# Chunked linear attention with an FFN: from a 128-token chunk step to a 64-token one, four more dummy products, and a new order of all pieces

## The chip, the core and the metric

The kernel runs on one core of a Trainium2 chip. The metric is the device time of one execution in microseconds (us); the time before is the median of three runs. A profile is the trace of one execution; its span runs from the first to the last instruction.

## What is computed

The reference, cut to what matters. For each of 4 batches and 8 heads, 768 tokens go through a decayed linear attention with a state of 16 x 32; then come a layer norm without bias and a two-layer ReLU network with a residual. All inputs and outputs are fp32.

```python
for c in range(nc):                      # chunks of 32 tokens
    cum = np.cumsum(la, axis=-1)         # la = log of the clipped decay a
    L = np.exp(cum[..., :, None] - cum[..., None, :]) * causal
    M = np.einsum('bhin,bhjn->bhij', Cc, Bc) * L
    y_intra = np.einsum('bhij,bhjd->bhid', M, xc)
    y_inter = np.einsum('bhin,bhnd->bhid', Cc, state) * np.exp(cum)[..., None]
    y[:, :, sl] = y_intra + y_inter
    state = exp(sum(la)) * state + sum_j(Bc_j x_j decay_from_j)
xn = (x - mu) / np.sqrt(var + 1e-06) * g_ln          # x = y, heads side by side
out = x + np.maximum(xn @ w_ch1, 0.0) @ w_ch2
```

## The kernel before

The 768 tokens are cut into six blocks of 128 (t = 0 to 5), and each block holds all 4 batches and 8 heads. Batches are counted as v (2) x u (2), heads in four pairs q. The work of a block is a set of small functions, called pieces here, each with a short name. The text `ISSUE` lists every piece of every block with its engine (`v` VectorE, `a` ScalarE, `p` GpSimd, `s` the DMA queue of SyncE); it is written out by hand, and each engine executes its instructions in that order. So an instruction that waits holds up everything behind it on its engine.

The pieces of the attention, with their lines in the profile:

- `C`, `cm`, `B`: C and B are multiplied by running decay products, rows `ud` that a DMA spreads over the partitions through DRAM (`ro`, then `ld ud`); block 0 takes these rows from two TensorE products instead (`U`, `ur`, L325 and L330). `cm` holds C twice, once with the odd heads zeroed and once with the even ones.
- `G` (L381, TensorE): the products of C and B, one call for each u. A call has 8 products whose moving operand has 256 columns (the first 64 keys against all 128 queries, two heads) and 8 with 128 columns (the last 64 keys against the last 64 queries). They work on 32x64 tiles of the array, 8 tiles at a time. An fp32 product stands in the trace as two MATMUL instructions, so a call counts 32.
- `R` (L388, VectorE): G times the decay mask `WW`, 128x384, eight times a block. `W` (L162, ScalarE or GpSimd) writes a block's decays into `WW`; `ones` fills it once with the causal mask.
- `I` (L400, TensorE): the state's share of y, 128 columns each, 32 instructions a block. `V` (L415, TensorE): R times x, 128 instructions a block on 64x32 tiles, half of 128 columns and half of 64. `Z` (L427, TensorE): the block's addition to the state, 64 instructions of 64 columns; it writes into a spare third of the banks of y.
- `K`, `S`, `sb` (L432, L441, L445): the state is decayed, added to, and laid out in blocks for the next block's `I`. `be` (L361) scales B for `Z`.

The pieces of the network:

- y is copied out of PSUM (`y`), split into a high and a low fp32r part (`yh`, `yl`), multiplied with the weights' two parts (`h`, L510, six products of up to 512 columns), passed through the ReLU by ScalarE (`hh`, L516), split by VectorE (`hl`, L522) and multiplied with the second weights (`o`, L537 and L538). `T`, `tw`, `tc` bring y into token order for the norm and the residual.
- The weights arrive as 64-bit words and are decoded on the chip by `k0`, `kr` (ScalarE), `k2`, `k3` (VectorE) and `f` (L212), centred by TensorE products (`wc`, `wm`, with `gd` and `gm` as factors) and split (`wh`, `wl`).
- `e`, `x`, `so`, `sm`, `mb`, `sp`, `em` make the decays of all blocks once, near the start. `fill` is a product of zeros that only keeps TensorE busy.

All PSUM tiles come from one pool of eight banks, `banks`: a piece that needs a bank waits until the reader of an earlier tile has released one.

Of the kernel before, what the change touches and what calls it, by code (L numbers as in the profile page):

```python
# [8 lines left out]
F32 = mybir.dt.float32  # L9
# [35 lines left out]
C_COEF = C_COL + P // NH  # L45
C_ID = C_COEF + 3 * P // 4
# [6 lines left out]
def shape_constants():  # L53
# [18 lines left out]
    w = np.concatenate([w[:, 1, :HALF], w[:, 3, HALF:], w[:, 2, :HALF], w[:, 3, :HALF], w[:, 0]], axis=1)  # L72
# [5 lines left out]
def linear_attention_ffn(ctx, tc, xv, a, bt, bn, cn, w1, w2, consts, out):  # L78
# [9 lines left out]
    rp = pool("rp", 12)  # L88
# [6 lines left out]
    cfr = hp.tile([P, 3 * P], F32, tag="hh", name="cfr")  # L95
# [12 lines left out]
    AZ = cp.tile([P, NL + 1], F32, name="AZ")  # L108
    inv = cp.tile([P, NL], F32, name="inv")
    ini = cp.tile([P, NL], F32, name="ini")  # L110
# [3 lines left out]
    WW = [cp.tile([P, NH, PW], F32, name=f"WW{i}") for i in range(NU)]  # L114

# [9 lines left out]
    def load(what, *at, e=nc.sync):  # L125
# [13 lines left out]
        elif what in src:  # L139
# [6 lines left out]
            e.dma_start(dst, src[what][t])  # L146
# [38 lines left out]
    def masks(u, e=nc.scalar):  # L185
        copy(e, WW[u], causal.unsqueeze(1).to_broadcast([P, NH, PW]))

# [63 lines left out]
    emt = cp.tile([P, NT, NB], F32, name="emt")  # L251
    msum = cp.tile([NR, NT, NSUB + 1], F32, name="msum")
    mblk = cp.tile([NR, NB, NT * (NSUB + 1)], F32, name="mblk")
# [11 lines left out]
    def sums_to(what):  # L265
        parts = lambda w: w.rearrange("p t (v u h) -> p v t u h", u=NU, v=NV)
        if what == "p":
            sums[what] = e = banks.tile([P, NT, NR], F32, tag="bank", name="ep")
            todo = [(4 + j, v, parts(e)[:, j]) for j in range(2) for v in range(NV)]
        else:  # L270
            sums[what] = e = banks.tile([P, 4, NT, NU, NH], F32, tag="bank", name="ew")
            todo = [(i, v, e[:, i]) for i in range(4) for v in range(NV)]
        for i, v, dst in todo:
            nc.tensor.matmul(dst[HALF * v:HALF * (v + 1)], cfr[:, i * HALF:(i + 1) * HALF], parts(la)[:, v], start=True, stop=True)

    def decays_to(what):
        nc.scalar.activation(*((pend, sums[what]) if what == "p" else (wt, sums[what])), AF.Exp)
# [7 lines left out]
    def decays_of():  # L285
        nc.scalar.activation(msum, sums["s"][:, :, :NSUB + 1], AF.Exp)

    def apart(e=nc.gpsimd):

        e.tensor_tensor(out=mblk, in0=msum.rearrange("r t i -> r (t i)").unsqueeze(1).to_broadcast([NR, NB, NT * (NSUB + 1)]),  # L290
                        in1=selt[:, P:].unsqueeze(2).to_broadcast([NR, NB, NT * (NSUB + 1)]), op=ALU.mult)

    def spread():

        sums["d"] = emps = banks.tile([P, NB, NT, NSUB + 1], F32, tag="bank", name="emps")
        nc.tensor.matmul(emps.rearrange("p b t i -> p (b t i)"), selt[:, :P], mblk.rearrange("r b c -> r (b c)"), start=True, stop=True)
# [74 lines left out]
    def score(t, u):  # L371

        bs, cm = tiles["bs", t], tiles["cm", t]
        G = [banks.tile([P, 2, PW], F32, tag="bank", name=f"G{t}{u}{q}") for q in range(NQ)]
# [10 lines left out]
    def weighted(t, u, q):  # L385
        R = tiles["R", t, u, q] = rp.tile([P, 2, PW], F32, tag="R", name=f"R{t}{u}{q}")
        flat = lambda v: v.rearrange("p i k -> p (i k)")
        nc.vector.tensor_tensor(out=flat(R), in0=flat(tiles.pop(("G", t, u, q))), in1=flat(WW[u][:, 2 * q:2 * q + 2]), op=ALU.mult)  # L388

    def inter_products(t):  # L390

        c2 = tiles["c2", t].rearrange("p i k -> p (i k)")
        for u in range(NU):
            for g in range(KC):
                tiles["y", t, u, g] = banks.tile([P, NU + 1, P], F32, tag="bank", name=f"yps{t}{u}{g}")
        for u in range(NU):
# [5 lines left out]
    def value(t, u):  # L402

        x = tiles["x", t]
        if t == u == 0:
            for v in range(NV):
                for g in range(KC):
                    tiles["y", t, v, g] = banks.tile([P, NU + 1, P], F32, tag="bank", name=f"yps{t}{v}{g}")
        for j in range(2):
            at = slice(P, PW) if j else slice(0, P)  # L410
            for g in range(KC):
                for k in range(4):
                    for v in range(NV):
                        h, c, p = 4 * g + k, 32 * (k ^ 2 * v), slice(HALF * v, HALF * (v + 1))
                        nc.tensor.matmul(tiles["y", t, v, g][c:c + 32, u, HALF * j:], x[p, (j * NU + u) * NH + h], tiles["R", t, u, h // 2][p, h % 2, at],  # L415
                                         start=(t == u == j == 0), stop=(j == 1), skip_group_check=True)

    def carry(t):

        x, be = tiles["x", t], tiles["be", t]  # L420
        Z = tiles["Z", t] = [tiles["y", t, v, 0][:, NU] for v in range(NV)]
        for u in range(NU):
            for j in range(2):
                for q in range(NQ):
                    for v in range(NV):
                        h0, p = (j * NU + u) * NH + 2 * q, slice(HALF * v, HALF * (v + 1))
                        nc.tensor.matmul(Z[v][32 * q:32 * q + 32, u * 2 * HD:(u + 1) * 2 * HD], be[p, h0:h0 + 2].rearrange("p h n -> p (h n)"),  # L427
                                         x[p, h0:h0 + 2].rearrange("p h d -> p (h d)"), start=False, stop=(j == 1), skip_group_check=True)

    def kept(t, e=nc.vector):  # L430
        S = tiles["K", t] = p1.tile([P, NB, 2 * HD], F32, tag="K", name=f"K{t}")
        e.tensor_tensor(out=S, in0=tiles["S", t - 1], in1=emt[:, t].unsqueeze(2).to_broadcast([P, NB, 2 * HD]), op=ALU.mult)  # L432

    def state_of(t):
        S = tiles["S", t] = p2.tile([P, NB, 2 * HD], F32, tag="S", name=f"S{t}")
        for v, z in enumerate(tiles.pop(("Z", t))):
            s = S[:, v * NU:(v + 1) * NU].rearrange("p u d -> p (u d)")
            if t == 0:
                nc.scalar.copy(s, z)
            else:  # L440
                nc.vector.tensor_tensor(out=s, in0=z, in1=tiles["K", t][:, v * NU:(v + 1) * NU].rearrange("p u d -> p (u d)"), op=ALU.add)  # L441
# [219 lines left out]
```

## Time and profile before

| | us |
|---|---|
| median of 3 runs | 190.68 (190.58 to 190.86) |
| the profiled execution: its time | 190.03 |
| the profiled execution: span of its instructions | 188.3 |
| TensorE busy | 181.6 (96% of the span) |
| VectorE, ScalarE, GpSimd busy | 134.5, 72.9, 51.6 |

The profile's page gives for each engine the time in which it executed something. The span and the time differ by 1.7 us, which lie before the first and after the last instruction. The granted TensorE clock averages 0.997 of full speed.

### The profile page before, as it was taken

The page shows a single profiled execution, that of the slowest core. Times are in us where ns is not written, and L with a number is a line of the kernel's source. Part 1 is how long each engine was busy: PE and PEld are TensorE (multiplying, and loading weights), DVE is VectorE, ACT ScalarE, POOL GpSimd, SP SyncE. Part 2 cuts the span into 40 slices and gives each one's busy share as a digit, 9 for nine tenths or more (in the row PEclk, how much of TensorE's full clock was granted, in tenths as well). Part 3 has the DMA queues.
Part 4 walks back from the last instruction along what each step waited for, and adds up shares of the span by engine and source line. Part 5 has one row for each costly group of instructions (what it writes and reads, how often), then busy time and mean ns, then how long its engine had stood idle before and what let it go on. Part 6 is the DMA issues. An engine that isn't in the chain of part 4 may idle for free.

```text
span 188.3 us, 5714 instructions
## 1 busy us (share of the span) xinstructions
PE 181.6 (96%) x2440; PEld 148.6 (79%) x2440; DVE 134.5 (71%) x302; ACT 72.9 (39%) x148; POOL 51.6 (27%) x65
## 2 busy tenths in 40 slices
PE   8979999999999999999998999999999999999992
PEld 8655589987878778788776887888888888888892
DVE  4899999998986797776984846659607574545841
ACT  7799999719434124421341201233102330034100
POOL 3162646624978941230032530000002000000000
PEclk9999999999999999999999999999999999999998
DMA  5999993843883913572150000363001035100102
GB/s 188 410 370 251 334 376 139 216 136 93 292 285 97 215 42 139 173 252 88 44 151 7 3 0 28 109 193 91 3 0 56 31 141 139 35 20 3 56 28 84
DMA packets 16729, 25.04 MB, mean 133 GB/s; under 512 B 4160, under 2 KB 10688, under 8 KB 16704
## 3 DMA queue, kind: packets, MB, share of 16 engines
q1 hardware_dynamic: 16560, 24.45, 40.3%
q8 instruction: 19, 0.31, 0.7%
q10 hardware_dynamic: 144, 0.23, 0.3%
q14 instruction: 6, 0.05, 0.1%
HBM read 18.06 MB, written 6.62 MB: 131 GB/s over the span
## 4 chain that ended last, share of the span: by engine, by line
PE 92%; ACT 4%; DVE 1%; issue 1%
PE ph L510 37%; PE po L537 23%; PE po L538 12%; PE yps L415 6%; PE G L381 4%; PE idle L556 2%; PE yps L427 2%; PE yps L400 2%; DVE R L388 1%; PE wc L226 1%; PE po L534 1%; ACT WW L162 1%; PE wc L227 1%; ACT raw L207 1%; ACT yh L162 1%
## 5 line engine op out<-in xcount | busy, mean ns | idle before, releaser
L537 PE MATMUL po<-w,hh 128*128 128x512 f32 x184 | 64.9, 396 | 0.1
L516 ACT ACTIVATE hh<-ph 128x512 fp32r<-128x512 f32 (+1 forms) x56 | 28.3, 536 | 74.0 <-PE ph L510 48.9
L510 PE MATMUL ph<-yh,w 128*128 128x512 f32 (+1 forms) x224 | 54.6, 365 | 0.0
L538 PE MATMUL po<-w,hl 128*128 128x256 f32 x184 | 47.9, 281 | 0.0
L522 DVE SCALAR_TENSOR_TENSOR hl<-ph,hh 128x512 fp32r<-128x512 f32 (+1 forms) x56 | 32.2, 604 | 17.1 <-ACT hh L516 17.1
L510 PEld LDWEIGHTS ph<-yh,w 128*128 128x128 f32 x224 | 38.2, 189 | 7.1 <-issue 0.3
L537 PEld LDWEIGHTS po<-w,hh 128*128 128x128 f32 x184 | 33.7, 188 | 7.1 <-ACT y L162 0.4
L538 PEld LDWEIGHTS po<-w,hl 128*128 128x128 f32 x184 | 34.7, 188 | 1.7
L510 PE MATMUL ph<-yl,w 128*128 128x512 f32 (+1 forms) x112 | 31.2, 360 | 0.0
L388 DVE TENSOR_TENSOR R<-G,WW 128x384 f32<-128x384 f32 x48 | 24.6, 546 | 5.6 <-PE G L381 4.9
L547 DVE SCALAR_TENSOR_TENSOR o<-po,rstd,ytok 128x256 f32<-128x256 f32 x24 | 11.5, 477 | 21.2 <-PE po L537 19.1
L510 PEld LDWEIGHTS ph<-yl,w 128*128 128x128 f32 x112 | 20.0, 189 | 3.5
L162 POOL COPY WW<-wt 32x512 f32<-32x512 f32 (+1 forms) x15 | 10.4, 695 | 17.0 <-DVE R L388 16.4
L162 POOL CAST yh<-y 128x512 fp32r<-128x512 f32 x5 | 3.3, 676 | 40.9 <-PE ph L510 33.5
L381 PE MATMUL G<-cm,bs 32*64 32x256 f32 (+1 forms) x384 | 12.0, 335 | 1.7 <-DVE bs L351 1.0
L162 ACT COPY WW<-wt 32x512 f32<-32x512 f32 (+1 forms) x21 | 12.8, 614 | 0.9 <-DVE rstd L501 0.7
L381 PEld LDWEIGHTS G<-cm,bs 32*64 32x64 f32 x384 | 7.4, 131 | 6.0 <-issue 2.4
L212 POOL TENSOR_TENSOR top<-top,raw 128x512 int32<-128x512 int32 x6 | 8.1, 1361 | 14.3 <-ACT WW L162 4.5
L547 DVE SCALAR_TENSOR_TENSOR o<-po,rstd,o 128x256 f32<-128x256 f32 x23 | 11.1, 484 | 0.8
L415 PEld LDWEIGHTS yps<-R,xt 64*32 64x32 f32 x768 | 10.1, 105 | 2.0 <-issue 1.2
L415 PE MATMUL yps<-R,xt 64*32 64x64 f32 (+1 forms) x768 | 11.2, 249 | 0.0
L490 DVE BATCH_NORM_STATS2 st<-ytok 128x6 f32<-128x256 f32 x24 | 9.4, 415 | 0.0
(100 smaller groups left out, 178.2 us busy)
## 6 DMA issues: line engine op xcount, KB each, us to landing
raw<-in_w_dram SPq DMA_DIRECT2D x8, 512.0 KB, 6.1
xt<-in_x_dram SPq DMA_DIRECT2D x6, 512.0 KB, 6.0
scr<-yx SPq DMA_DIRECT2D x6, 512.0 KB, 2.9
ytok<-scr SPq DMA_DIRECT2D x24, 128.0 KB, 3.0
out_dram<-o SPq DMA_DIRECT2D x24, 128.0 KB, 1.7
ud<-scr SPq DMA_DIRECT2D x10, 256.0 KB, 4.0
c<-in_cn_dram SPq DMA_DIRECT2D x6, 256.0 KB, 4.7
b<-in_bn_dram SPq DMA_DIRECT2D x6, 256.0 KB, 3.9
```

The costliest lines, as they stand in the source:

```text
L162: (e.copy if e is nc.scalar else e.tensor_copy)(dst, src)
L212: e.tensor_tensor(out=f, in0=f, in1=words.pop((w, *at))[0], op=ALU.add)
L381: nc.tensor.matmul(G[q][HALF * v:HALF * (v + 1), :, at], bs[r, i0 + HALF * j:i0 + HALF * (j + 1)], cm[r, :, i0 + HALF * j:i0 + P], start=T ...
L388: nc.vector.tensor_tensor(out=flat(R), in0=flat(tiles.pop(("G", t, u, q))), in1=flat(WW[u][:, 2 * q:2 * q + 2]), op=ALU.mult)
L415: nc.tensor.matmul(tiles["y", t, v, g][c:c + 32, u, HALF * j:], x[p, (j * NU + u) * NH + h], tiles["R", t, u, h // 2][p, h % 2, at], start ...
L490: nc.vector.bn_stats(out=st, in_=tiles["ytok", t][:, :, b])
L510: nc.tensor.matmul(ph, W1[m // 4, k][:, s, mc], v[:, k, tok], start=(i == 0), stop=(i == len(cmb) - 1))
L516: nc.scalar.activation(tiles["hh", t, m][:, tok], tiles["ph", t, m, u], AF.Relu)
L522: nc.vector.scalar_tensor_tensor(out=tiles["hl", t, m][:, tok], in0=tiles.pop(("ph", t, m, u)), scalar=0.0, in1=tiles["hh", t, m][:, tok]. ...
L537: both = lambda: nc.tensor.matmul(po, hh, w[:, :, at], start=(m == 0), stop=last, skip_group_check=True)
L538: low = lambda: nc.tensor.matmul(po[:, 0], hl, w[:, 0, at], start=False, stop=False, skip_group_check=True)
L547: nc.vector.scalar_tensor_tensor(out=parts(o), in0=parts(po[:, i]), scalar=tiles["rstd", t][:, b], in1=rest, op0=ALU.mult, op1=ALU.add)
```

## The change

**Blocks 1 to 5 in two halves of 64.** `G` becomes one call a block with 32 products of 128 columns (64 instructions): each 64 queries meet only their own 64 keys. `R` becomes four steps of 128x512, with a mask `WC` that serves all of these blocks; `W` becomes two copies a block in place of six. The earlier keys reach a query through the state, which now has two values a block: `I` multiplies the first 64 queries with the state at the block's start and the last 64 with the state in its middle (64 instructions of 64 columns). `V` becomes 128 instructions of 64 columns, in two calls split by half of the heads. `Z` fills both halves into two PSUM banks of its own; `K`, `S` and `sb` run twice a block. Block 5 gets a `Z` (half), `K`, `S`, `sb` and `be` that it didn't have. Block 0 keeps the old scheme.

**Near the start.** `U` makes 128 columns in place of 512, and `ur` four products of 128 in place of one of 512 (with a new step `rg` on GpSimd). A new step `on` fills `WC` with the causal mask, once on each of VectorE and ScalarE. `ones` stands on ScalarE for both u (one was on VectorE). There are 17 `fill` in place of 13. Several tiles now share the buffers of later ones, and the pool of `R` has 8 buffers in place of 12.

**The order.** `ISSUE` is new as a whole. The core of the diff:

```diff
-            todo = [(i, v, e[:, i]) for i in range(4) for v in range(NV)]
-        for i, v, dst in todo:
-            nc.tensor.matmul(dst[HALF * v:HALF * (v + 1)], cfr[:, i * HALF:(i + 1) * HALF], parts(la)[:, v], start=True, stop=True)
+            todo = [(i, v, slice(0, NT if i < 2 else 1), e[:, i]) for i in range(4) for v in range(NV)]
+        for i, v, t, dst in todo:
+            nc.tensor.matmul(dst[HALF * v:HALF * (v + 1), t], cfr[:, i * HALF:(i + 1) * HALF], parts(la)[:, v, t], start=True, stop=True)
...
+    def decays(t, u=None, e=nc.scalar):
+        if t:
+            for p in (slice(0, SUB), slice(HALF, HALF + SUB)):
+                dst = WC[p].rearrange("p u q (i j k) -> p (u q i) j k", i=2, j=2)[:, :, :, SUB:]
+                src = wt[p, :2, t].rearrange("p j u h -> p (u h) j")
+                copy(e, dst, src.unsqueeze(3).to_broadcast([*src.shape, SUB]))
+            return
...
+    def score(t, u=None):
 
         bs, cm = tiles["bs", t], tiles["cm", t]
+        if t:
+            G = [banks.tile([P, NU, 2, P], F32, tag="bank", name=f"G{t}{q}") for q in range(NQ)]
+            for j in range(2):
+                for u in range(NU):
+                    for q in range(NQ):
+                        r = slice(2 * DS * q, 2 * DS * (q + 1))
+                        for v in range(NV):
+                            at = slice((v * NU + u) * P + HALF * j, (v * NU + u) * P + HALF * (j + 1))
+                            nc.tensor.matmul(G[q][HALF * v:HALF * (v + 1), u, :, HALF * j:HALF * (j + 1)], bs[r, at], cm[r, :, at], start=True, stop=True)
...
-        for u in range(NU):
-            for q in range(NQ):
-                for v in range(NV):
-                    b, r, f = v * NU + u, slice(2 * DS * q, 2 * DS * (q + 1)), slice((q ^ v) % 2 * 2 * HD, ((q ^ v) % 2 + 1) * 2 * HD)
-                    nc.tensor.matmul(tiles["y", t, v, q // 2][f, u], tiles["sbd", t - 1][r, b], c2[r, b * P:(b + 1) * P], start=(u == 0), stop=False, skip_group_check=True)
+        summed(t)
+        for j in range(2):
+            state = tiles["sbd", t, 0] if j else tiles["sbd", t - 1, 1]
+            for u in range(NU):
+                for q in range(NQ):
+                    for v in range(NV):
+                        b, r, f = v * NU + u, slice(2 * DS * q, 2 * DS * (q + 1)), slice((q ^ v) % 2 * 2 * HD, ((q ^ v) % 2 + 1) * 2 * HD)
+                        nc.tensor.matmul(tiles["y", t, v, q // 2][f, u, HALF * j:HALF * (j + 1)], state[r, b], c2[r, b * P + HALF * j:b * P + HALF * (j + 1)],
+                                         start=(u == j == 0), stop=False, skip_group_check=True)
...
-        Z = tiles["Z", t] = [tiles["y", t, v, 0][:, NU] for v in range(NV)]
+        Z = tiles["Z", t] = [banks.tile([P, 2, P], F32, tag="bank", name=f"Z{t}{v}") for v in range(NV)]
         for u in range(NU):
-            for j in range(2):
+            for j in range(1 if t == NT - 1 else 2):
...
-ld:s w1 1 1, k3:v 1 0 0, f:p 1 0 0, fill 12, G 0 1, W:a 0 0, e p, k3:v 1 0 1, k0 1 1 1, k0 2 0, R 0 1 0, f:p 1 0 1, kr 1 1 1, R 0 1 2, G 0 0,
+fill 14, fill 15, W:p 0 1, ld:s w1 1 1, ld:s w1 1 0, on:a 0, k0 1 1 1, k2:v 1 1 1, ld:s late, ld:s w2 0, e p, x p, fill 16, G 0 1, gm:p, k3:v 1 0 0,
```

What the new order does at three places follows as rows of instructions, each engine's in its own order; the number behind a tile's name only tells buffers apart, and line numbers differ between the two kernels. First ScalarE from its first copy on. `WW` from `causal` (`early` in the changed kernel) is `ones`, the step on `cst` is the logarithm of the decays, `top` is `k0` and `raw` is `kr` of the weights. Before:

```order
L162 COPY WW_89<-causal 128x1536
L162 CAST cfr<-cst 128x384
L263 ACTIVATE cst<-cst 128x192
L162 COPY uds<-uds 128x160
L193 ACTIVATE top_142<-raw_137 128x512
L277 ACTIVATE wt<-ew 128x384
L207 ACTIVATE raw_137<-raw_137 128x512
L220 ACTIVATE gd<-cst,gneg 128x128 x2
```

The same place in the changed kernel:

```order
L169 COPY WW_88<-early 128x1536
L169 CAST cfr<-cst 128x448
L169 COPY WW_87<-early 128x1536
L273 ACTIVATE cst<-cst 128x192
L203 ACTIVATE top_134<-raw_106 128x512
L169 COPY uds<-uds 128x160
L217 ACTIVATE raw_106<-raw_106 128x512
L203 ACTIVATE top_179<-raw_127 128x512
L217 ACTIVATE raw_127<-raw_127 128x512
L290 ACTIVATE wt<-ew 128x192
```

A second copy of the mask now stands ahead of the logarithm and of the first `k0`. Next VectorE between the first decay products and block 0's `bs`, on which `G` of block 0 waits (`own` or `own_ini` is `U`, `top` is `k2`, `k3` and `f`). Before:

```order
L325 TENSOR_TENSOR own_159<-uds,cst 128x512
L314 SCALAR_TENSOR_TENSOR uds<-AZ,inv 128x192
L197 TENSOR_SCALAR top_142<-top_142 128x512
L325 TENSOR_TENSOR own_166<-uds,cst 128x512
L341 SCALAR_TENSOR_TENSOR cm_170<-c_162,cst,rows_168 128x512 x2
L197 TENSOR_SCALAR top_182<-top_182 128x512
L351 TENSOR_TENSOR bs_187<-b_180,rows_185 128x512
```

The same place in the changed kernel:

```order
L343 TENSOR_TENSOR own_ini<-uds,cst 128x128
L328 SCALAR_TENSOR_TENSOR uds<-ends 128x192
L207 TENSOR_SCALAR top_134<-top_134 128x512
L169 COPY uds<-uds 128x160
L343 TENSOR_TENSOR own_ini<-uds,cst 128x128
L212 SCALAR_TENSOR_TENSOR top_134<-raw_106,top_134 128x512
L207 TENSOR_SCALAR top_179<-top_179 128x512
L222 ISA top_134<-raw_106,top_134 128x1024
L361 SCALAR_TENSOR_TENSOR cm_193<-c_191,cst,rows_154 128x512 x2
L371 TENSOR_TENSOR bs_196<-b_129,rows_186 128x512
```

Two more weight steps and a copy now stand ahead of `cm` and `bs`, and the two `U` are a quarter as wide. Last TensorE at block 1's first `G`, behind the last product of an `h` (`ph`). Before:

```order
L510 MATMUL ph_503<-yl_394,w_287 128x256
L381 MATMUL G_517<-cm_478,bs_501 64x2x128 x2
L381 MATMUL G_518<-cm_478,bs_501 64x2x128 x2
L381 MATMUL G_519<-cm_478,bs_501 64x2x128 x2
L381 MATMUL G_520<-cm_478,bs_501 64x2x128 x2
L381 MATMUL G_517<-cm_478,bs_501 64x2x64 x2
L381 MATMUL G_518<-cm_478,bs_501 64x2x64 x2
L381 MATMUL G_519<-cm_478,bs_501 64x2x64 x2
L381 MATMUL G_520<-cm_478,bs_501 64x2x64 x2
```

The same place in the changed kernel, where the last four rows come four times in all:

```order
L566 MATMUL ph_559<-yl_407,w_325 128x256
L409 MATMUL G_572<-cm_505,bs_527 64x2x64 x2
L409 MATMUL G_573<-cm_505,bs_527 64x2x64 x2
L409 MATMUL G_574<-cm_505,bs_527 64x2x64 x2
L409 MATMUL G_575<-cm_505,bs_527 64x2x64 x2
```

The wide products of 256 columns are gone, and block 1 has this one call in place of two. In the changed kernel six `h` calls and `Z` of block 0 stand between block 0's `V` and this `G`; before, `Z` and four `h` calls did. From there on TensorE meets the small pieces in stretches with `h` or `o` between them: 15 stretches before, and 15 in the changed kernel from this `G` on plus `Z` of block 0.

## Rows read from the trace of the kernel before

**Rows 1.** The page's first part: busy us (share of the span) xinstructions.

```profile
PE 181.6 (96%) x2440; PEld 148.6 (79%) x2440; DVE 134.5 (71%) x302; ACT 72.9 (39%) x148; POOL 51.6 (27%) x65
```

**Rows 2.** Waits of TensorE over the span: us in total, times, longest.

```profile
PE G L381 <- issue: 0.7, 1, 0.7
```

**Rows 3.** Timeline of TensorE, 10 to 26 us: start, us, instruction xcount [idle before].

```profile
10.10 0.91 PE L381 MATMUL G<-cm,bs 32*64 32x256 f32 x32 [0.95 <-DVE bs L351]
...
13.70 1.12 PE L226 MATMUL wc<-top,gd 128*128 128x512 f32 x2 [0.40 <-POOL top L212]
...
17.33 1.82 PE L415 MATMUL yps<-R,xt 64*32 64x128 f32 x128
19.24 1.98 PE L232 MATMUL wm<-top,gneg 128*128 128x512 f32 x4
21.47 1.12 PE L427 MATMUL yps<-xt,be 64*32 64x64 f32 x64 [0.25 <-ACT yh L162]
22.52 0.74 PE L510 MATMUL ph<-yh,w 128*128 128x256 f32 x4
...
25.78 0.91 PE L381 MATMUL G<-cm,bs 32*64 32x256 f32 x32
26.70 0.45 PE L296 MATMUL emps<-mblk,cst 32*128 32x120 f32 x2
```

**Rows 4.** Timeline of TensorE in blocks 2 and 4.

```profile
60.46 0.86 PE L427 MATMUL yps<-xt,be 64*32 64x64 f32 x64
61.25 0.91 PE L381 MATMUL G<-cm,bs 32*64 32x256 f32 x32
62.08 1.20 PE L510 MATMUL ph<-yh,w 128*128 128x512 f32 x4
...
63.67 0.91 PE L381 MATMUL G<-cm,bs 32*64 32x256 f32 x32
...
126.85 1.07 PE L510 MATMUL ph<-yh,w 128*128 128x512 f32 x4
...
128.21 1.07 PE L510 MATMUL ph<-yh,w 128*128 128x512 f32 x4
...
129.66 0.69 PE L400 MATMUL yps<-c,sbd 32*64 32x128 f32 x32
130.28 1.82 PE L415 MATMUL yps<-R,xt 64*32 64x128 f32 x128
132.03 1.20 PE L510 MATMUL ph<-yh,w 128*128 128x512 f32 x4
```

**Rows 5.** Timeline of ScalarE from its first copy on.

```profile
2.16 1.47 ACT L162 COPY WW<-causal 128x1536 f32<-128x1536 f32 x1
...
4.33 0.36 ACT L263 ACTIVATE cst<-cst 128x192 f32<-128x192 f32 x1
...
5.27 0.67 ACT L193 ACTIVATE top<-raw 128x512 f32<-128x512 f32 x1
```

**Rows 6.** Timeline of VectorE up to block 0's first R.

```profile
6.19 0.40 DVE L197 TENSOR_SCALAR top<-top 128x512 int32<-128x512 int32 x1
...
7.66 1.41 DVE L341 SCALAR_TENSOR_TENSOR cm<-c,cst,rows 128x512 f32<-128x512 f32 x2 [0.47 <-PE rows L330]
...
9.36 0.68 DVE L351 TENSOR_TENSOR bs<-b,rows 128x512 f32<-128x512 f32 x1
...
11.35 2.88 DVE L388 TENSOR_TENSOR R<-G,WW 128x384 f32<-128x384 f32 x6
```

**Rows 7.** Groups of instructions of VectorE and GpSimd by shape: busy us, mean ns of one.

```profile
L441 DVE TENSOR_TENSOR S<-yps,K 128x128 f32<-128x128 f32 x8 | 1.9, 278 | 0.1
...
L432 POOL TENSOR_TENSOR K<-S,emt 128x256 f32<-128x256 f32 x3 | 2.3, 765 | 0.0
```

**Rows 8.** DMAs issued between 6 and 9.3 us, KB, us to landing; and what they moved.

```profile
DMA packets 443, 1.36 MB, mean 411 GB/s; under 512 B 48, under 2 KB 48, under 8 KB 443
...
xt<-in_x_dram SPq DMA_DIRECT2D x1, 512.0 KB, 8.3
```

More of the change, by code (lines that the diff above doesn't have):

```diff
@@ L145, in load @@
                 dst = tiles[what, t] = p2.tile([P, TB], F32, tag="b" + what, name=f"{what}{t}")
-            e.dma_start(dst, src[what][t])
+            cols = slice(0, TB // 2 if (what, t) == ("bt", NT - 1) else dst.shape[1])
+            e.dma_start(dst[:, cols], src[what][t][:, cols])
         elif what == "w1":
@@ L387, in weighted, with summed @@
         flat = lambda v: v.rearrange("p i k -> p (i k)")
         nc.vector.tensor_tensor(out=flat(R), in0=flat(tiles.pop(("G", t, u, q))), in1=flat(WW[u][:, 2 * q:2 * q + 2]), op=ALU.mult)
+    def summed(t):
+        for v in range(NV):
+            for g in range(KC):
+                tiles["y", t, v, g] = banks.tile([P, NU, P], F32, tag="bank", name=f"yps{t}{v}{g}")
     def inter_products(t):
         c2 = tiles["c2", t].rearrange("p i k -> p (i k)")
-        for u in range(NU):
-            for g in range(KC):
-                tiles["y", t, u, g] = banks.tile([P, NU + 1, P], F32, tag="bank", name=f"yps{t}{u}{g}")
@@ L404, in value @@
+    def value(t, part):
         x = tiles["x", t]
[L405 to L408, printed above, removed]
+        if t == part == 0:
+            summed(t)
         for j in range(2):
             at = slice(P, PW) if j else slice(0, P)
-            for g in range(KC):
+            for i in range(2):
+                u, g = (i, part) if t else (part, i)
@@ L434, in state_of, with kept @@
[L434 to L436 removed]
+                        nc.tensor.matmul(Z[v][32 * q:32 * q + 32, j if t else 1, u * 2 * HD:(u + 1) * 2 * HD], be[p, h0:h0 + 2].rearrange("p h n -> p (h n)"),
+                                         x[p, h0:h0 + 2].rearrange("p h d -> p (h d)"), start=(u == j == 0), stop=(j == 1 or t > 0), skip_group_check=True)
+    def kept(t, j, e=nc.vector):
+        K = tiles["K", t, j] = p1.tile([P, NB, 2 * HD], F32, tag="K", name=f"K{t}{j}")
+        e.tensor_tensor(out=K, in0=tiles["S", t, 0] if j else tiles["S", t - 1, 1], in1=emt[:, t, j].unsqueeze(2).to_broadcast([P, NB, 2 * HD]), op=ALU.mult)
@@ L437, in state_of @@
+    def state_of(t, j):
+        S = tiles["S", t, j] = p2.tile([P, NB, 2 * HD], F32, tag="S", name=f"S{t}{j}")
+        for v, z in enumerate(tiles["Z", t]):
             s = S[:, v * NU:(v + 1) * NU].rearrange("p u d -> p (u d)")
             if t == 0:
-                nc.scalar.copy(s, z)
+                nc.scalar.copy(s, z[:, j])
             else:
-                nc.vector.tensor_tensor(out=s, in0=z, in1=tiles["K", t][:, v * NU:(v + 1) * NU].rearrange("p u d -> p (u d)"), op=ALU.add)
-    def diagonal(t, e=nc.gpsimd):
-        sb = tiles["sbd", t] = p2.tile([P, NB, 2 * HD], F32, tag="sbd", name=f"sbd{t}")
-        e.tensor_tensor(out=sb, in0=tiles["S", t], in1=blkt.unsqueeze(1).to_broadcast([P, NB, 2 * HD]), op=ALU.mult)
+                nc.vector.tensor_tensor(out=s, in0=z[:, j], in1=tiles["K", t, j][:, v * NU:(v + 1) * NU].rearrange("p u d -> p (u d)"), op=ALU.add)
@@ L447, in gathered, with diagonal @@
+    def diagonal(t, j, e=nc.gpsimd):
+        sb = tiles["sbd", t, j] = p2.tile([P, NB, 2 * HD], F32, tag="sbd", name=f"sbd{t}{j}")
+        e.tensor_tensor(out=sb, in0=tiles["S", t, j], in1=blkt.unsqueeze(1).to_broadcast([P, NB, 2 * HD]), op=ALU.mult)
     def gathered(t, u, g, e=nc.scalar):
```

185 lines of the change are left out of this document (105 added, 80 removed).

## Prediction

> **What bounds the kernel now.** I read the busy time of the engines first: TensorE works for 181.6 of the 188.3 us of the span, VectorE for 134.5, the others for less [rows 1]. Then the waits of TensorE: past the first 22 us only one of note is left, 0.7 us in front of a `G` with no releaser shown [rows 2]. So from the first `h` on the time is the sum of TensorE's pieces, and what the change does there is counted at full price. Last the timeline of the front, where TensorE does wait: 0.95 us for block 0's `bs`, 0.40 for a weight step on GpSimd, 0.25 before `Z` [rows 3]. There VectorE and ScalarE set the end, and a step put in their way counts.
>
> **A price for small products.** I take pieces from their start to the next one's start, since the ends are modelled. `G` takes 0.83 (61.25 to 62.08), `Z` 0.79, `I` 0.62, `V` 1.75 [rows 4]. `I` issues 32 x 128 = 4096 columns, a `G` call 16 x 256 + 16 x 128 = 6144. Two thousand columns more cost 0.21 us, so an estimate is 0.20 us for a piece plus 0.105 for each 1024 columns, and nothing for an instruction. `Z` bounds it: its 64 products of 64 columns are 4096 columns too, yet take 0.17 more than `I`. So products of 64 columns are charged by count: (0.79 - 0.20) / 64 = 9.2 ns each. `V` gives a second reading: 1.75 less 0.20 and less 0.84 for its 64 products of 128 columns leaves 0.71 for 64 of 64 columns, 11.1 ns each.
>
> **Blocks 1 to 5 on TensorE.**
> `G`: one call of 64 x 128 = 8192 columns, 0.20 + 8 x 0.105 = 1.04, in place of two of 0.83: -0.62 (I take -0.61).
> `I`: 64 products of 64 columns, 0.79 (as `Z`) to 0.91 (at 11.1 ns) in place of 0.62: +0.17 to +0.29, taken +0.2.
> `V`: two calls of 64 products of 64 columns, 2 x 0.79 = 1.58 to 2 x 0.91 = 1.82 in place of 1.75: -0.17 to +0.07. I take -0.17, because `Z` is the same shape on the same 64x32 tiles.
> Per block -0.58 (-0.63 to -0.25), for five -2.9 (-3.15 to -1.25).
> Block 5's new `Z` has 32 such products: 0.20 + 32 x 9.2 ns = 0.49, at the higher price 0.55: +0.5.
> The number of stretches of small products between full-size ones goes from 15 to 16. An `h` between two small pieces takes 1.59 (62.08 to 63.67), among its like 1.36 (126.85 to 128.21) [rows 4]: +0.2 for the one more.
> TensorE's work changes by -2.9 + 0.5 + 0.2 = -2.2, bounds -2.45 and -0.5.
>
> A rule of the Trainium skill speaks against halving columns. The page "TensorEngine Tiling (Array Packing)", section "Instruction Overhead", says that a product costs about 60 cycles however few columns it has, and that one shouldn't take a tiling factor from a dimension already small. Read as a charge on each instruction in a row, 60 cycles at 2.4 GHz are 25 ns, and `V`'s 128 instructions would last 3.2 us; they last 1.75, so here at most the tiles that work side by side can each pay it. By that reading the sum would be about +12 us; by the rows it is the one above.
>
> **The front.** On ScalarE a second mask copy, 1.47 us like the first, stands ahead of the logarithm, which started at 4.33 [rows 5] and now starts at about 5.8. The first `k0` stood behind the logarithm and a copy of the decay rows; that copy now stands behind `k0` on ScalarE, and a second one like it on VectorE. The result of `k0` was there at 5.27 + 0.67 = 5.94 and now comes at about 6.8. On VectorE the row of steps up to `bs` was `k2` (0.40, from 6.19), `U`, then after `ur` two `cm` (1.41) and `bs` (0.68, end 10.04) [rows 6]. The new row begins about 0.8 later and holds a second `k3`-and-`k2` pair (0.65 + 0.40, the first of them an estimate from the two-operand steps of 0.68) and a short `f` ahead of `cm`; against that `U` is a quarter as wide and no 0.47 us wait for the rows stands ahead of `cm`. I come to `bs` ending at 11.3 and `G` of block 0 at 11.35, 1.25 later than 10.10 [rows 3]. The four more dummy products stand ahead of this `G`, in time in which TensorE waits for `bs` anyway.
>
> That lateness should end within the weights. Block 0's first `wc` was held until 13.70 by an `f` that GpSimd made alone [rows 3]; it is now shared with VectorE, and I expect `wc` at 13.6. `R` begins 1.25 after `G` as before, so at 12.6, and at the spacing of six in 2.88 us [rows 6] all eight are done at 16.5, before `V` wants them. `V` comes at 13.6 + 3.63 for the `wc` products (13.70 to 17.33) + 0.45 for the `sp` product, which moved ahead of it [rows 3] = 17.7. `wm` then ends at 21.5, and the first `h` can start there: 1.0 before the 22.52 of now. `Z` of block 0 (0.8) is still owed then and `sp` (0.45) is not, so the front gives 1.0 - 0.8 + 0.45, about -0.6. That holds if the steps of VectorE and ScalarE follow each other at the trace's spacing; if each lasts its full printed duration, they add 1.6 and it is +1.0. Taken: -0.4, near the first end, because the `R`s of this same stretch do follow at 0.48.
> Block 0's x load is moved behind two loads of 768 KB together, about 1.9 us at the 411 GB/s of that stretch. Issued at 6, it took 8.3 us [rows 8] and landed near 14.4; at 16.3 it is still ahead of `V` at 17.7, so free; beyond 1.4 us more it would be paid in full.
>
> **New waits.** The state in the middle of a block now lies between `Z` and `I` of the same block: `S` twice 0.278 on VectorE, `K` 0.765 on GpSimd, `S` twice again, with the block layout `sb` and the bank releases behind it [rows 7]: about 1.9 us. In blocks 2 to 5 over 5 us of `h` or `o` stand between the two, which hides it. In block 1 three half `h` (0.72 each, 2.16) stand there, while VectorE still has a queue of weight steps: a wait of 0 to 1.2 us, taken +0.4. A wait on VectorE for `Z` would hold its `hl` splits, and so the `o` products. The pieces taken off other engines (20 `W` copies and 20 `R` steps less; an `R` of 512 in place of two of 384) lie beside TensorE's work and count nothing.
>
> **Sum.** -2.2 (products) - 0.4 (front) + 0.4 (waits) = -2.2, against the profiled execution's 190.03: 187.8. The median of the runs is 0.65 above that execution, and I shift by the same: 188.5. The same as a milestone: `G` of block 1 starts at 25.78 [rows 3]; in the changed kernel TensorE's work behind that point is 4.3 us less (`G` 3.05, `V` 0.85, two half `h` 1.44, `sp` 0.45, less `I` 1.0 and `Z` 0.5), so it may start up to 30.1 before the gain is gone, and I expect 27.8.
>
> **The rivals.**
> B, the front goes at its best, block 1 doesn't wait and the 0.7 us in front of a `G` [rows 2] goes with the call that it stood before: 190.7 - 2.2 - 0.6 - 0.5 = 187.4. For it: all other waits are short. Chance 0.12.
> C, the front costs its full durations (+1.0) and block 1 its full wait (+1.2): -2.2 + 2.2 = 0, 190.7. For it: the front is a chain in which each step waits for another engine's, so what one loses the next can't win back. Chance 0.13.
> D, slower: `G` of block 1 waits for its four banks. They are released by ScalarE's copies of y, which stand behind the new `WC` copies, some 1.0 us each (two thirds of 1.47 [rows 5]), and `Z` now holds two banks of its own. From a start of `G` past 30.1 this decides; I price 31, which gives 191.5. Against it: nothing but `V` needs those copies, and ScalarE is busy for 72.9 of 188.3 us only [rows 1]. Chance 0.10.
> E, products are charged by count alone, at `V`'s (1.75 - 0.20) / 128 = 12.1 ns also for 128 columns, and longer ones by their share. Then `G` gains only the 0.20 of a call (-1.0 in all), `V` loses that 0.20 (+1.0), `I` grows by 0.39 (+1.95), `Z` costs 0.6: +2.55 + 0.2, so about 193.4. Against it: a `G` call of 32 instructions takes 0.83, a `Z` of 64 takes 0.79. Chance 0.04.
> F, the 64-column products all cost the upper price of 11.1 ns: -0.5 for the products, 190.2. For it: `V`'s own half of that width gave this price [rows 4]. Chance 0.06.
> The forecast, 188.5 with 187.6 to 189.6 of its own: 0.55.
>
> **How the numbers follow.** About 0.2% (0.38 us) is what a measurement of this kernel tells from no change. Faster holds the forecast, B, half of F and a little of C: 0.75. Slower holds D, E and some of C that goes beyond its price: 0.13; the rest, 0.12, is same. The range 187.0 to 190.6 leaves out the far part of B, and D, E and part of C, about 0.2.
>
> **What would show it.** In the changed kernel's timeline of TensorE: `G` of blocks 1 to 5 at 1.05, `I` at 0.8, each `V` call at 0.79, block 5's `Z` at 0.5; `G` of block 0 at 11.35, `V` at 17.7, the first `h` at 21.5, `G` of block 1 at 27.8. Wrong would be: a wait of over 1.2 us between 24 and 42 us (D), a `V` call of 0.9 or more (F), an `I` above 1.0 (E), or a first `h` later than 23 (C).

## The result, and the profile after

The changed kernel takes 187.93 us (median of 20 runs) against 190.54 for the kernel before in the same runs; the ratio is 0.9845 (95% interval 0.9816 to 0.9874), a gain of 2.4 to 3.5 us. The ratio is of the fast runs alone, of the changed kernel 14 of the 20, which reach from 186.49 to 188.77; the two medians of all runs would give 0.986. The forecast was 188.5 (187.0 to 190.6) and "faster". The number is right; the front and the waits came out differently from the text, and the experiments are mostly about these.

The profiled execution of the changed kernel took 188.36 us, 0.4 above the median. The first part of its page, with the header line and the queue that loads instructions:

```profile
span 186.6 us, 6136 instructions
...
PE 180.9 (97%) x2656; PEld 151.7 (81%) x2656; DVE 130.6 (70%) x292; ACT 72.2 (39%) x143; POOL 57.4 (31%) x65
...
q8 instruction: 21, 0.34, 0.8%
```

Its waits of TensorE over the whole span, as in [rows 2] (total, times, longest):

```profile
PE idle L612 <- PEq L705: 0.8, 1, 0.8
PE rows L350 <- DVE own_ini L343: 0.8, 1, 0.8
PE msps L297 <- DVE R L434: 0.6, 1, 0.6
```

After 16 us no wait is left, neither the predicted one in block 1 nor the 0.7 of [rows 2]. Next comes the timeline of TensorE (start, us, instruction), of which [rows 3] and [rows 4] showed the pieces before. L350 is `ur`, L420 and L471 are `G` and `V` of block 0; L409, L451, L468 and L483 are `G`, `I`, `V` and `Z` of the later blocks:

```profile
6.22 2.05 PE L350 MATMUL rows<-own_ini,rg 128*128 128x128 f32 x8 [0.79 <-DVE own_ini L343]
...
13.08 1.63 PE L420 MATMUL G<-cm,bs 32*64 32x256 f32 x64
...
19.93 1.82 PE L471 MATMUL yps<-R,xt 64*32 64x128 f32 x128
...
29.50 1.21 PE L409 MATMUL G<-cm,bs 32*64 32x128 f32 x64
30.64 0.74 PE L566 MATMUL ph<-yh,w 128*128 128x256 f32 x4
...
56.33 0.91 PE L451 MATMUL yps<-c,sbd 32*64 32x64 f32 x64
57.17 0.86 PE L468 MATMUL yps<-R,xt 64*32 64x64 f32 x64
57.96 1.20 PE L566 MATMUL ph<-yh,w 128*128 128x512 f32 x4
...
108.05 0.54 PE L483 MATMUL Z<-xt,be 64*32 64x64 f32 x32
108.52 1.22 PE L409 MATMUL G<-cm,bs 32*64 32x128 f32 x64
```

Read from start to next start, `G` takes 1.14 (29.50 to 30.64), `I` 0.84, a `V` call 0.79, block 5's `Z` 0.47. `G` of block 1 starts at 29.50, where it started at 25.78. So this execution loses 3.7 us ahead of that point and gains 162.5 - 157.1 = 5.4 behind it.

### The profile page after: what moved, and what is told of

Read it like the earlier page. It is cut to its first block, busy times and chain, and to the rows that moved or that the text cites. A ratio compares the mean times of both kernels' runs of the same rounds, so it can differ in the third digit from the quotient of the medians.

```text
span 186.6 us, 6136 instructions
## 1 busy us (share of the span) xinstructions
PE 180.9 (97%) x2656; PEld 151.7 (81%) x2656; DVE 130.6 (70%) x292; ACT 72.2 (39%) x143; POOL 57.4 (31%) x65
## 4 chain that ended last, share of the span: by engine, by line
PE 90%; DVE 3%; ACT 2%; DMA 2%; issue 1%
PE ph L566 35%; PE po L593 23%; PE po L594 12%; PE yps L468 4%; PE G L409 3%; PE yps L451 2%; DMA cst<-in_consts_dram 2%; PE rows L350 2%; PE Z L483 2%; PE wc L236 1%; PE po L590 1%; PE idle L612 1%; PE wc L237 1%; PE yps L471 1%; DVE o L603 1%
## 5 line engine op out<-in xcount | busy, mean ns | idle before, releaser
L603 DVE SCALAR_TENSOR_TENSOR o<-po,rstd,ytok 128x256 f32<-128x256 f32 x24 | 11.5, 478 | 20.0 <-PE po L593 14.2
L522 POOL TENSOR_TENSOR yl<-y,yh 128x512 fp32r<-128x512 f32 x7 | 9.9, 1411 | 29.0 <-ACT yh L169 14.9
L429 DVE TENSOR_TENSOR R<-G,WC 128x512 f32<-128x512 f32 x20 | 13.2, 675 | 0.1
L603 DVE SCALAR_TENSOR_TENSOR o<-po,rstd,o 128x256 f32<-128x256 f32 x23 | 11.1, 484 | 0.8
L169 ACT COPY y<-yps 128x256 f32<-128x256 f32 x18 | 6.3, 382 | 13.8 <-PE yps L468 13.8
L169 DVE COPY y<-yps 128x256 f32<-128x256 f32 x6 | 2.5, 415 | 9.2 <-PE yps L468 9.2
L530 DVE STREAM_TRANSPOSE yx<-y 128x512 f32<-128x512 f32 x12 | 8.4, 699 | 0.0
L468 PE MATMUL yps<-R,xt 64*32 64x64 f32 x640 | 8.4, 224 | 0.0
L169 ACT COPY WC<-wt 32x1024 f32<-32x1024 f32 x8 | 8.3, 1040 | 0.0
L468 PEld LDWEIGHTS yps<-R,xt 64*32 64x32 f32 x640 | 6.9, 105 | 1.6 <-issue 1.2
L612 PE MATMUL idle<-const-float32-0.0 128*128 128x128 f32 x34 | 7.1, 380 | 0.8 <-PEq L705 0.8
```

What stands on the lines that cost most here:

```text
L169: (e.copy if e is nc.scalar else e.tensor_copy)(dst, src)
L429: nc.vector.tensor_tensor(out=R.rearrange("p (u k) -> p u k", u=NU), in0=tiles.pop(("G", t, q)).rearrange("p u i k -> p u (i k)"), in1=WC[ ...
L468: nc.tensor.matmul(tiles["y", t, v, g][c:c + 32, u, HALF * j:HALF * (j + 1)], key, tiles["R", t, h // 2][p, u, h % 2, HALF * j:HALF * (j + ...
L522: e.tensor_tensor(out=tiles["yl", t][:, :, tok], in0=tiles["y32", t][:, :, tok], in1=tiles["yh", t][:, :, tok].bitcast(F32), op=ALU.subtract)
L603: nc.vector.scalar_tensor_tensor(out=parts(o), in0=parts(po[:, i]), scalar=tiles["rstd", t][:, b], in1=rest, op0=ALU.mult, op1=ALU.add)
L612: nc.tensor.matmul(banks.tile([P, P], F32, tag="bank", name=f"idle{i}"), zero.to_broadcast([P, P]), zero.to_broadcast([P, P]), start=True, ...
```

## The experiments

All are edits of the changed kernel but e10, which edits the kernel before. Ratios are against the kernel before in the same runs, to be held against 0.9845. In the texts of e1 to e3 theory 2 is the prediction's account of the front. The rate of TensorE that they speak of is the spacing of its products; e5 says more on it.

**e1: two dummy products ahead of ur.**

```diff
-fill 9, k2:v 1 0 1, rg:p, ur 0, ... fill 10, fill 11, kr 1 0 1, fill 12
+fill 9, fill 10, fill 11, k2:v 1 0 1, rg:p, ur 0, ... kr 1 0 1, fill 12
```

> Two of the dummy products that stand between block 0's first rows products (ur) and the second go ahead of the first; 17 in all, nothing else changes. Theory 1 (the 0.79 us in which TensorE is idle before ur keeps its products at the half rate, 213 ns for 128 columns, until 10.0 us): with the idle time filled the rate doubles near 6 us as in the kernel before, ur takes 0.9 instead of 1.98, the second ur starts near 9.0 instead of 10.43, G of block 0 near 11.4 instead of 13.08, and the time falls by 1.2 to 1.7 us. Theory 2 (that of the prediction: the mask copy on ScalarE ahead of the logarithm makes the front late, dummy products are free): nothing changes by more than 0.2 us.

187.78, ratio 0.9868 (0.983 to 0.9907). `ur` lasted 1.05 and `G` of block 0 started at 11.13, but TensorE's rate had already doubled at 3.9 us, ahead of the edit's place, and the idle time was 1.07. So this is no test of theory 1. The front was earlier and the time was the same.

**e2: the four added dummy products out.** `fill 12` to `fill 15` are left out.

> The four added dummy products are taken out (13 are left: ten ahead, two between the two ur, one ahead of G of block 0). Theory 1 (they stand on the chain: ur, dummies, second ur, bs, and dummies, ep, dummy, G): the second ur starts 0.2 to 0.35 us earlier, G of block 0 0.8 to 1.2 us earlier, at 11.9 to 12.3, and some 0.8 of it reaches the time, unless the rate of TensorE falls back. Theory 2 (that of the prediction, they lie in time in which TensorE waits anyway): G of block 0 and the time stay within 0.2 us.

188.75, ratio 0.9864 (0.981 to 0.9919). `G` at 11.10, after a wait of 0.5 for `bs`: within 0.4 of the kernels with all 17 (11.32, 11.39 and 11.49 in e4, e3 and e8). Taken out alone, the added ones are worth next to nothing: `bs` is there no earlier.

**e3: the mask copy late.**

```diff
-ones:a 0, l1, l2, ... kr 1 0 0, x w, f:v 1 0 1
+l1, l2, ... kr 1 0 0, ones:a 0, x w, f:v 1 0 1
```

> The second mask copy on ScalarE goes behind the first weight steps, so the logarithm and the first k0 stand where they did before the change. Theory 2 (that of the prediction: this copy makes the front late): k0, the logarithm and the steps behind them come 1.2 to 1.4 us earlier, G of block 0 about 0.8 us earlier, the time falls by about 0.8. Theory 1 (ur waits for U, and U for a VectorE step that GpSimd's rg holds up, not for ScalarE): ur still starts at 6.2 with the idle 0.8 ahead of it, G of block 0 stays at 13.1 within 0.2, the time within 0.3.

187.92, ratio 0.9885 (0.9842 to 0.9928). The logarithm came at 4.30 in place of 5.66, yet `ur` started at 6.24 with the same idle 0.8 ahead of it, and the time did not fall. `bs` did come earlier. In e8, which has the changed kernel's program up to here, it ended at 11.3:

```profile
10.66 0.68 DVE L371 TENSOR_TENSOR bs<-b,rows 128x512 f32<-128x512 f32 x1
```

In e3 it ended at 10.7, but `G` followed only at 11.39, without idle time, behind TensorE's own row of `ur`, dummy products and `ep`:

```profile
10.01 0.68 DVE L371 TENSOR_TENSOR bs<-b,rows 128x512 f32<-128x512 f32 x1
...
11.39 1.63 PE L420 MATMUL G<-cm,bs 32*64 32x256 f32 x64
```

So the mask copy holds `bs` by up to 0.65, and that is worth nothing while TensorE's own row is as long. With the dummy products out (e2) it is `bs` that `G` waits for. No run changes both.

**e4: rg on VectorE.**

```diff
-clip, u, iv, ... k2:v 1 0 1, rg:p, ur 0
+clip, rg:v, u, iv, ... k2:v 1 0 1, ur 0
```

> The new step rg is made by VectorE, right behind the step that clips the decays, instead of by GpSimd. Theory 1 (GpSimd's rg, 3.93 to 4.97, holds up VectorE's step on 128x186, which lasts 1.10 us where it lasted 0.25): that step is back at about 0.25, rg costs VectorE 0.65, U ends and ur starts 0.2 to 0.4 us earlier, the idle time before ur falls to 0.4 to 0.6 us; the time moves by at most 0.5. Theory 2 (the long step is a late load of the decays): it stays at about 1.1 us, ur starts 0.65 later.

187.32, ratio 0.9843 (0.9806 to 0.9879). VectorE's step behind the clipping, first in the changed kernel, with GpSimd's `rg` beside it:

```profile
3.99 1.10 DVE L319 TENSOR_SCALAR ends<-a 128x186 f32<-128x186 f32 x1
...
3.93 1.04 POOL L338 TENSOR_TENSOR rg<-cst 128x512 f32<-128x512 f32 x1 [1.73 <-DMA cst<-in_consts_dram]
```

and then in e4:

```profile
4.05 0.25 DVE L319 TENSOR_SCALAR ends<-a 128x186 f32<-128x186 f32 x1
4.21 0.68 DVE L338 TENSOR_TENSOR rg<-cst 128x512 f32<-128x512 f32 x1
```

In the changed kernel that step ends 0.12 us after GpSimd's; without `rg` beside it, it takes 0.25. That held `U`: in e4 `ur` started at 5.91, 0.3 earlier, and the idle time ahead of it fell from 0.8 to 0.6. The Trainium skill, page "SBUF — State Buffer", section "SBUF: two separate sides", says that GpSimd and certain VectorE instructions take a shared pair of ports as an exclusive lock, held for a whole instruction. The 1.10 and 0.25 agree with it.

The fronts of e1 to e4 are 1.7 to 2.0 us earlier at `G` of block 0 than the profiled execution of the changed kernel, and the times hardly differ. In e1, e2 and e4 a new wait shows where this goes, at block 3's `Z`:

```profile
PE Z L483 <- DVE hl L578: 0.8, 1, 0.8
```

```profile
PE Z L483 <- DMA xt<-in_x_dram: 2.3, 1, 2.3
```

```profile
PE Z L483 <- DVE R L429: 1.4, 1, 1.4
```

The names differ, the cause does not: the load of block 3's x was issued at 60.20, 61.85 and 59.48 and took 6.1, 6.4 and 7.1 us, landing at 66.3, 68.2 and 66.6; each time `Z` started 0.13 to 0.14 us later. In the changed kernel's profile it landed at 67.03, and `Z` started at 67.16 behind `G`, just in time. The load stands in SyncE's queue behind `tc 1`, which waited 5.3 to 6.0 us for a write to land. In e3 it was issued at 58.74, landed at 65.3, and `Z` did not wait.

**e5: block 3's x early.**

```diff
-ld:s ud 3 1, yh:p 1 1, ... R 3 2, ld:s x 3, ld:s ud 4 1
+ld:s ud 3 1, ld:s x 3, yh:p 1 1, ... R 3 2, ld:s ud 4 1
```

> The load of block 3's x moves ahead in the DMA queue, from behind tc 1, od and ud 4 to right behind ud 3 1; nothing else changes. Up to block 1 this is the changed kernel itself, so its front is a second look at that one. Theory 3 (an earlier front is given back at Z of block 3, which waits until this load has landed at 66 to 68 us): in the profile Z of block 3 follows G of block 3 without a wait; if ur again runs at the full rate (near 6.3 to 7.3 us, as in three of the other kernels) the span is 184 to 184.5, and the median falls by 0.8 to 1.6 us against the 187.3 to 187.9 of the kernels measured so far. Theory 4 (what Z of block 3 waits for comes later anyway, the steps R or S of VectorE): the wait stays, or comes back within 10 us, and the time stays within 0.4 us. On the half rate of the front: if it belongs to the change, ur lasts 2.0 us again and G of block 0 starts near 13.1; if it was this one execution, ur lasts 1.0 and G of block 0 starts near 11.3.

188.28, ratio 0.9876 (0.9832 to 0.9921). `Z` of block 3 followed `G` without a wait, but this profile was no test of theory 3, since its front was late, and the median did not fall:

```profile
6.23 2.05 PE L350 MATMUL rows<-own_ini,rg 128*128 128x128 f32 x8 [0.80 <-DVE own_ini L343]
...
10.84 1.91 PE L350 MATMUL rows<-own_ini,rg 128*128 128x128 f32 x8
...
14.56 1.63 PE L420 MATMUL G<-cm,bs 32*64 32x256 f32 x64
```

Both `ur` ran at the half rate: 213 ns from product to product of 128 columns, the lower of TensorE's two levels (1.2 GHz), where the upper (2.4 GHz) has 112. The trace also records the granted clock, and in every profile its first record of the full clock begins where the spacing falls: at 5.1 to 5.9 in e2, e3, e4 and e8 (in the last dummy product ahead of `ur` or the idle time behind it), at 7.0 in e6, at 10.0 in the changed kernel's profile and at 13.1 in e5 and e7. Up to `ur` TensorE's program is the same in the changed kernel, e2, e3, e5, e7 and e8. So it is the execution and not an edit that sets it, and in these six it moves `V` of block 0 between 18.3 and 21.2.

**e6: e4 and e5 together.**

> Both edits together: rg on VectorE and the load of block 3's x early. Theory 3: rg on VectorE brought G of block 1 to 27.59, but Z of block 3 then waited 1.4 us; without that wait the span is 185.8 - 1.4 = 184.4 and the time about 186.2. Theory 4: 187.3 again.

186.96, ratio 0.9822 (0.9784 to 0.9861). No wait is left behind 15 us. From `G` of block 1 (28.29) to the last product (181.88) are 153.6 us; in e4, from 27.59 to 182.55, 155.0. The difference is the 1.4 that `Z` waited there, so theory 3 holds for the wait. The time of 186.2 was not reached: the front was 0.7 later than e4's, with the rate doubled at 7.0 and 0.9 of waiting for `R`. The intervals of e4 and e6 overlap.

**e7: G twice.**

```diff
-            for j in range(2):
+            for j in (0, 1, 0, 1):
```

> Every G call of blocks 1 to 5 issues its 64 products twice into the same banks (the output is the same, the work is not): five times 64 instructions more, at 64 x 14.9 ns = 0.95 us each. If TensorE's work is what the time consists of, the time rises by 4.8 us. If Z of block 3 waits for a load at a fixed time, the three G ahead of it (2.9 us) fill that wait of up to 1.4 us first, and the time rises by 3.4 to 4.0. If the products wait for weights or for other engines, by less than 2.5.

201.18, ratio 1.0539 (1.0484 to 1.0595): 13 us more than the changed kernel, where 4.8 was the most expected. A `G` with 128 products took 2.03, 0.89 more than one with 64 (13.9 ns for each more, where 14.9 was expected), so five explain 4.5. The profiled execution, at 203.24 the slowest of four, shows the rest in the waits of TensorE:

```profile
PE Z L483 <- issue: 3.0, 2, 1.6
PE G L409 <- issue: 2.6, 2, 1.5
PE po L593 <- issue: 1.3, 1, 1.3
PE yps L468 <- issue: 1.2, 1, 1.2
```

These are six stops with no releaser, 8.1 us. Three stand in stretches of 192 to 224 small products in a row, the others in the `Z` and the `V` of block 1 and in an `o` 4 us behind that `V`. The queue of instruction loads:

```profile
q8 instruction: 23, 0.38, 0.8%
```

The kernel before has 19 of these packets, the changed one 21. It is the kind of stop that stood in [rows 2]: there the stretch of `I 4`, `V 4 0`, `Z 4`, `G 5 0` and `V 4 1` has 256 small products in a row, and `G 5 0` in it took 2.21 (100.42 to 102.63) in place of 0.84:

```profile
100.42 0.65 PE L381 MATMUL G<-cm,bs 32*64 32x256 f32 x4
101.81 0.90 PE L381 MATMUL G<-cm,bs 32*64 32x256 f32 x28 [0.74 <-issue]
102.63 1.05 PE L415 MATMUL yps<-R,xt 64*32 64x128 f32 x64
```

The longest stretch of the changed kernel has 160.

The trace has the time of each packet, and this ties the stops to the loading of instructions. Over all profiles there are ten stops without a releaser, of 0.4 us or more: one in the kernel before, one in e3, six here and two in e8. Each of the ten ended 1.26 to 1.61 us after a packet of this queue had ended, while the packets come 3 to 26 us apart. What fills these 1.3 to 1.6 us is not shown.

**e8: I in products of 32 columns.** Each product of `I` in blocks 1 to 5 is cut in two.

> I of blocks 1 to 5 is cut once more: 128 products of 32 columns in place of 64 of 64 (same output). By count at the 11.3 ns that one of 64 columns took: a call lasts 0.15 + 128 x 11.3 ns = 1.6 in place of 0.86. By columns alone it stays at 0.86. At 25 ns for each instruction, the floor that the Trainium skill gives for one behind another, 3.3. In between, with a lower floor than at 64 columns (7 ns): 1.05.

197.49, ratio 1.037 (1.031 to 1.043). Block 2's `I` and the next `V`:

```profile
56.78 1.89 PE L453 MATMUL yps<-c,sbd 32*64 32x32 f32 x128
58.59 0.86 PE L470 MATMUL yps<-R,xt 64*32 64x64 f32 x64
```

`I` lasts 1.82 for 128 products, above the 1.6 by count: halving 64 columns saves nothing per product, it doubles their number. The price by instruction is 14 ns, not the 25 of the Trainium skill, page "TensorE: Matmul & The Clock Gate", section "Wait — 56ns, not 53.3ns?"; with tiles side by side that floor does not hold from one instruction to the next. Five `I` explain 4.8 us of the 9.6; stops without a releaser, 3.0 more. A third part is the granted clock, in the page's row of 40 slices (in tenths of full speed):

```profile
PEclk9999999999999999999999699999999999999999
```

By the trace's record it was at half from 108.0 to 111.4, beginning 0.1 us after a stop of 1.4 us. The `o` products between that `V` and the next took 7.1 there, 5.8 in the changed kernel: 1.3 more. The rest is unexplained.

**e9: no idle time before ur.** As e6, and `fill 10` and `fill 11` ahead of `ur 0` as in e1.

> rg on VectorE, block 3's x early, and two of the dummy products that stood behind the first ur ahead of it (17 in all), which at the half rate keep TensorE busy to about 6.1 us, past the end of U. If the idle time before ur is what lets the half rate last to 7, 10 or 12.5 us in some executions, the rate has doubled by 6.2 us in this profile, ur lasts 0.9 to 1.1, G of block 1 starts at 27.6 or earlier, and the times of the runs lie closer together: median 186.0 to 186.6, all below 188. If the moment at which the rate doubles has nothing to do with that gap, it lies anywhere from 4 to 12.5 us again and the times spread as before.

186.85, ratio 0.9823 (0.9796 to 0.9851), all five runs between 186.18 and 187.35. That is a spread of 1.2, where the changed kernel's 14 have 2.3; but e4, with the gap, has 1.3 in six, so the spread decides nothing. The fills at half rate last to the start of `ur`, and the rate doubled right there, at 5.9:

```profile
6.01 1.07 PE L350 MATMUL rows<-own_ini,rg 128*128 128x128 f32 x8
...
18.14 1.81 PE L471 MATMUL yps<-R,xt 64*32 64x128 f32 x128 [0.50 <-DMA xt<-in_x_dram]
```

That agrees with theory 1 of e1. So do the other profiles: where no idle time stands ahead of `ur` (the kernel before, e10 and this one) the rate doubled at 5.9 to 6.5, and all four that doubled later (7.0 to 13.1) had 0.5 to 0.8 of it. But six with such a gap doubled by 5.9, so three profiles can't show that it never happens late without one. The ratios of e9 and the changed kernel overlap.

**e10: the kernel before, its longest stretch cut.**

```diff
-h 2 1, hh 2 1, hl 2 1, I 4, V 4 0, Z 4, cm:a 5 0, G 5 0, ... V 4 1, y:a 4 1 0
+I 4, V 4 0, h 2 1, hh 2 1, hl 2 1, Z 4, V 4 1, cm:a 5 0, G 5 0, ... y:a 4 1 0
```

> The kernel before, with its longest stretch of small products cut: h 2 1 goes between V 4 0 and Z 4, and V 4 1 ahead of G 5 0, so that 96 and 160 small products follow each other where 256 did. If the 1.38 us that one G of the kernel before lost there (2.21 in place of 0.84, no releaser shown) come from TensorE's instructions not arriving fast enough in so long a stretch, that G lasts 0.84, no gap without releaser above 0.3 us is left, and the time falls by 1.0 to 1.4 us: that much of the change's gain came from this. If it was an accident of that execution or moves with the instructions, a gap of 0.5 to 1.5 us stands elsewhere and the time is the same within 0.4.

189.59, ratio 0.9973 (0.9948 to 0.9998). The stretch falls into 96 and 160 products. `G 5 0` is back to its normal length and the stop without a releaser is gone; a wait for a bank took part of its place:

```profile
PE po L537 <- DVE R L388: 0.8, 1, 0.8
```

So the order of the small products does matter: by the ratio 0.5 us is gained of the 1.4, with an interval that ends just short of no change, and the bank wait that the new order makes takes most of the rest. With the packets' times (e7) this bears out that in the stops TensorE's instructions arrive late. The length of one stretch is not the whole of it, since three of e7's stops stand outside long ones.

**e11: four R ahead of a weight step.** As e9, `k2:v 1 1 0` behind `R 0 1 3`.

> As e9_no_gap, and the first four R of block 0 go ahead of a weight step (k2) for which VectorE waits. With rg on VectorE, R started 1.95 us after G of block 0, and TensorE waited 0.9 us for it (msps, which needs R's bank). Here R should start 0.8 to 1.2 us after G, that wait fall below 0.2, and the time fall by up to 0.7 against e9_no_gap, if nothing of the weights becomes late: wc must not wait more than 0.3 for its weights.

187.27, ratio 0.9843 (0.9816 to 0.987). `wc` started at 13.41 against 13.50 in e9, which did not have the wait either: nothing to win, and no difference that can be told.

## Why the prediction was right

**Products.** The mechanism was right, the sizes partly. `G` was put at 1.04 and took 1.14 (1.36 in block 4, with a pause of the kind of e7's stops): its saving over five blocks is 2.4, not 3.05. `I` cost +1.2 where +1.0 was taken, two `V` calls 1.58 as taken (1.41 back to back in block 1), block 5's `Z` 0.47. Together, `V` first, -1.0 - 2.4 + 1.2 + 0.5 = -1.7, against -2.4 for these terms. The failing assumption is the column model: a product of 128 columns follows the one before at 14.9 ns, not at the 13 of 0.105 per 1024 columns.

**The 0.7 without a releaser.** The forecast left it out, rival B gave it 0.5. It was worth 1.38 at its `G`, and is gone in the changed kernel. This more than made up for the mis-sized `G`. Three misses met behind block 1's `G`: 0.7 less from the products, 1.4 more from this stop, 0.4 more from a wait that did not come. That the sum came out near is in part luck. With the stop and the work that moved ahead (two half `h`, `sp`) the pieces give 5.0 of the 5.4 gained behind block 1's `G`. No run has the halves of 64 without the new order, so what the order alone is worth is not shown.

**The front.** Its forecast, `G` at 11.35, `V` at 17.7 and block 1's `G` at 27.8, is where the executions with an early rate are (11.1 to 11.6, 17.9 to 19.2 and 27.4 to 28.7). The reason was half right. With the mask copy ahead, `bs` ended at 11.0 to 11.3 where 11.3 was forecast, and at 10.7 without it. The step that failed is "in time in which TensorE waits for `bs` anyway": TensorE's own row with the dummy products lasts to 11.1 to 11.5 (e1, e3, e4, e8), so that neither e2 nor e3 moves `G` by more than 0.4. With both edits `G` might start near 10.7, an estimate from e3's `bs` and the end of e2's row at 10.6. GpSimd's `rg`, not counted at all, adds 0.85 to a step of VectorE, of which 0.3 reached `ur` and 0.2 `G` (11.49 in e8, 11.32 in e4). The profiled execution shows 13.08 and 19.93, since there TensorE stayed at its lower level until 10.0; the forecast has no term for that. Also wrong was "at 16.3 it is still ahead of `V`": block 0's x was issued at 9.8 to 11.1. It landed at 16.1 in the changed kernel's profile but at 17.6 to 19.7 in those of the experiments, and where the front was early `V` of block 0 waited 0.4 to 0.8 for it (e1, e2, e3 and e9).

**New waits.** "Taken +0.4" in block 1 was wrong by place: there is none. One of 0.8 to 2.3 us stands at block 3's `Z` in e1, e2 and e4 (not in e3 and e8, whose front was early too), under the sentence "in blocks 2 to 5 over 5 us of `h` or `o` stand between the two, which hides it": that looked at the state and not at the x load. It gives back 0.8 and 1.4 of the 1.9 by which the front was early in e1 and e4, and all of the 1.3 in e2.

**The rivals.** C's late front did occur in the profile (29.5, near its 30.1), without its wait in block 1. D, E and F did not: there was no wait for `G`'s banks, a `G` of 128 columns was cheaper per block than before, and `V` came at the lower price (10.2 ns a product); only `I` came at F's upper one (11.1 to 11.7).

Beyond both kernels, e6 and e9 have the lowest medians, 186.96 and 186.85; against the changed kernel this is not more than the measurement can tell.

## What to carry to other kernels

Price small products by the instruction as well as by the column, and ask how fast TensorE uses up its instructions. `G` and `V` lost a third of their columns and became 31% and 10% shorter; `I`, cut from 128 columns to 64 at the same total, became 38% longer, and at 32 columns its time doubled again. When an early stage is sped up, look for the next load with a fixed place in a DMA queue before counting the gain. A GpSimd step beside VectorE's chain is not free just because GpSimd is idle.

## What the runs showed of the hardware

- TensorE's products went from 213 to 112 ns per 128 columns at 5.4 to 13.1 us in six kernels whose TensorE does the same up to `ur`. The trace's first record of the full clock begins there (5.42, 5.60, 5.90, 9.99, 13.06 and 13.10). The page counts the time ahead of that record as full speed, so neither its PEclk row nor its mean (0.997 before, 1.000 after) shows the lower level there.
- TensorE made stops of 0.4 to 1.6 us without a releaser among many small products; 320 products more brought 8 us of them (e7) or 3 us (e8). All ten ended 1.26 to 1.61 us after a packet of the instruction queue.
- Products of 64 columns followed each other at 10.2 ns on 64x32 tiles and at 11.1 to 11.7 on 32x64 tiles, those of 32 columns on 32x64 tiles, two in a row on one tile, at 13.2, and those of 128 columns on 32x64 tiles at 14.9.
